# Attention into a mixture of four attention experts: both heads of a row through DRAM in one tile

## The chip, the cores and the metric

One core of one Trainium2 chip. The metric is the device time of one execution in microseconds (us), given as the median of several runs. The engines are TensorE (PE, with its weight loads as PEld), VectorE (DVE), ScalarE (ACT), GpSimd (POOL) and SyncE (SP), which here issues every DMA; its queue is SPq in the trace.

## The reference

Everything is float32. Causal attention over 8 heads with a window of 128 and 4 sink columns gives x; x goes through four experts of attention, whose outputs are weighted by the two best gates of each position.

```python
scores = scale * np.matmul(q, k.transpose(0, 1, 3, 2))          # q, k, v: (4, 8, 768, 64)
scores = np.where(is_sink | in_window, scores, -1e9)            # window 128, 4 sinks
a = softmax(scores); attn = np.matmul(a, v)
x = attn.transpose(0, 2, 1, 3).reshape(4, 768, 512)
...
logits = x @ w_gate; topk = the two largest of the 4 logits; w = softmax(their logits)
for e in range(4):
    q, k, v = x @ wq[e], x @ wk[e], x @ wv[e]                   # (4, 768, 64)
    a = softmax(where(causal, scale * q @ k.T, -1e9))
    ye = a @ v @ wo[e]
    out += (weight of e at this position, 0 if not chosen) * ye
```

## The kernel before

The work is cut into units. A unit `first(b, hp)` is the windowed attention of one batch and one pair of heads (16 of them), a unit `second(b, ep)` is the causal attention of one batch and one pair of experts (8 of them), with `values` (the projections of the values and the gates) before and `store` (the output projection) behind. The two heads or experts of a pair sit in the two halves of PE's rows, so one step does both. A unit has 6 rows of 128 positions; row i of a `second` sees i + 1 blocks of 128 columns. The stages of one such row in `wide_rows`: scores on PE (L1358), mask and minimum on DVE (L1571), exponential on ACT (L1579), sum and reciprocal (`factor`, L1413 to L1422), normalisation on POOL or ACT (`scaled`, L1238 or L1236), turning of the probabilities, product with the values on PE (`acc.add`, L1397), finisher.

The turning is done by PE with an identity (L1430) and copied out of PSUM, except in the rows named by `AWAY`: rows 3, 4 and 5 of the units (0,0), (0,1), (1,0), (1,1) and (2,0). Those go through DRAM in `by_way_of_dram`: for each of the two heads, the normalised probabilities are written in another order of columns into a tile `u` of the ring "p", DVE transposes it in blocks of 32 x 32 (L1523), one DMA writes it to a DRAM tile `there` (L1524), and four DMAs read it back so that the blocks of 32 rows change places (L1518). PE then multiplies with it directly, without transposes or copies.

Scores and trips share the ring "p" of 13 tiles of 768 columns; `there` is a ring of 4 tiles in DRAM, one per head.

The program of each engine is a list in a fixed order. `Plan.emit` makes it: each piece of work is a `Step` with a priority, modelled costs per engine it may run on, the steps it comes after and the ring buffers it takes or uses. `emit` goes through modelled time, gives each engine the step that can begin first (on PE: the least of priority plus `HURRY` times the wait, plus `STAY` and `BULK` terms where the tile mode changes), and writes the steps out in that order. `NUDGE` is a table of some 3000 numbers that shift the priorities of groups and of single steps, `ONLY` is a table that ties steps to one engine. On SP a step's `moves` is the modelled time that its bytes take. Where the model sees a gap on PE in the first 130 us, `fill` puts dummy products in (L1045). At run time the engines follow their lists and wait for each other by semaphores, so a wait in front of one instruction holds up all that stands behind it on its engine.

Of the kernel before, what the change touches and what calls it, by code (L numbers as in the profile page):

```python
# [39 lines left out]

FREE = {PE: 1100.0, DVE: 4500.0, ACT: 2100.0, POOL: 5300.0, SP: 790.0}

NUDGE = {
    "busy_PE": -19.1, " ": 0.5, " busy_PE": 42.4, " busy_PE 0": -148.0, "sink_values_DVE": 84.9, " sink_values_DVE": 10.8,
    " sink_values_DVE 0": -114.0, "load_SP": 37.3, " load_SP": 4.4, " load_SP 0": 5.1, "again_SP": 20.0, " again_SP": -6.7,
    "sink_values_ACT": -13.2, " sink_values_ACT": -20.4, " sink_values_ACT 0": 41.8, "sink_values_POOL": -7.2,
    " sink_values_POOL": 9.3, " sink_values_POOL 0": 10.1, "sink_values_SP": -9.6, " sink_values_SP": -26.6,
    " sink_values_SP 0": 39.2, " load_SP 1": -28.6, " weight_ACT": -0.4, " weight_ACT 0": 9.4, "weight_POOL": 6.6,
    " weight_POOL": -1.7, " weight_POOL 0": -35.7, " weight_ACT 1": 23.3, " weight_POOL 1": -20.8, " weight_ACT 2": 25.1,
# [1933 lines left out]
```

## Time and profile before

| what | value |
|---|---|
| median of 3 runs | 392.97 us (389.96 to 392.98) |
| the profiled execution | 394.25 us, its span 392.5 us |
| mean granted PE clock | 0.972 of full speed |
| busy, share of the span | PE 94%, PEld 81%, DVE 73%, ACT 70%, POOL 50% |
| HBM read and written | 30.88 and 16.12 MB |
| DMA issues through DRAM | 30 writes `there<-p`, 120 reads `p<-there` |

The span runs from the first to the last instruction of the profiled execution. A group's row has its busy time in us, the mean duration of one instruction in ns, and the idle time of the engine just before its instructions with what ended that. A busy PE is not PE at its peak, since the ends of matmuls are modelled.

### The profile page before, as it was taken

Reading aid. Unit: us, or ns where it says so; the run is one execution under the profiler, and the core shown is the slowest. Engines: PE = TensorE matmul, PEld = TensorE weight load, DVE = VectorE, ACT = ScalarE, POOL = GpSimd, SP = SyncE. Lnnn points to the kernel's source line nnn. Section 1 sums busy time; section 2 is a strip of 40 time slices with the busy share of each in tenths; the row PEclk is TensorE's granted clock in tenths of the full one; section 3 lists DMA queues with packets and bytes.
Section 4 is the critical chain, followed back from the end, with each engine's and each line's share of the span. In section 5 each row is a group of like instructions: output and inputs, shape, how many; then the busy total and the mean of one; then the engine's idle time right before and its main releaser. Section 6 shows DMA issues by size and latency. Waiting matters only on the chain.

```text
span 392.5 us, 13096 instructions
## 1 busy us (share of the span) xinstructions
PE 367.4 (94%) x4648; PEld 318.2 (81%) x4648; DVE 287.8 (73%) x1263; ACT 275.5 (70%) x950; POOL 196.0 (50%) x476
## 2 busy tenths in 40 slices
...
GB/s 165 205 154 151 161 188 171 115 0 130 212 198 112 124 243 152 91 60 301 198 156 136 135 222 154 19 3 183 249 177 2 3 28 28 2 1 109 3 55 109
DMA packets 145634, 48.13 MB, mean 123 GB/s; under 512 B 122976, under 2 KB 138336, under 8 KB 145568
## 3 DMA queue, kind: packets, MB, share of 16 engines
...
q8 instruction: 37, 0.61, 0.7%
q14 instruction: 29, 0.24, 0.2%
HBM read 30.88 MB, written 16.12 MB: 120 GB/s over the span
## 4 chain that ended last, share of the span: by engine, by line
PE 57%; DMA 12%; SPq 10%; DVE 9%; ACT 6%; issue 3%; POOL 2%; DVEq 0%; ACTq 0%; POOLq 0%
PE b L1397 12%; PE b L1800 10%; PE b L1874 9%; PE b L1827 8%; PE b L1358 6%; PE b L1430 6%; SPq L1518 5%; SPq L1768 3%; DMA qn<-in_q_dram 3%; DMA there<-p 3%; PE b L1371 2%; DMA p<-there 2%; PE b L1353 2%; ACT p L1579 1%; DVE p L1571 1%
## 5 line engine op out<-in xcount | busy, mean ns | idle before, releaser
L1579 ACT ACTIVATE p<-p,st 128x128 f32<-128x128 f32 (+5 forms) x96 | 63.7, 666 | 6.1 <-DVE st L1571 4.8
L1709 ACT ACTIVATE p<-p,st 128x132 f32<-128x132 f32 x128 | 50.7, 401 | 9.3 <-DVE st L1705 9.1
L1571 DVE CUSTOM_DVE_ANT_0 p<-b,cmask 128x384 f32<-128x384 f32 (+3 forms) x96 | 45.5, 502 | 2.3 <-PE b L1358 1.9
L1358 PE MATMUL b<-ks,qs 64*128 64x384 f32 (+3 forms) x384 | 44.4, 349 | 0.8 <-DVE y L1215 0.6
L1430 PE MATMUL b<-ident,p 64*128 64x64 f32 x820 | 40.1, 229 | 4.7 <-DVE st L1705 2.6
L1430 PEld LDWEIGHTS b<-ident,p 64*128 64x128 f32 x820 | 33.8, 141 | 10.9 <-issue 3.2
L1227 ACT ACTIVATE pt<-b 128x256 f32<-128x256 f32 (+3 forms) x102 | 38.7, 417 | 5.3 <-PE b L1430 4.5
L1397 PE MATMUL b<-pt,vn 128*64 128x128 f32 x448 | 41.2, 289 | 0.4 <-ACT pt L1227 0.4
L1413 POOL TENSOR_TENSOR st<-st 128x4 f32<-128x4 f32 (+1 forms) x57 | 11.3, 200 | 56.7 <-ACT p L1579 34.6
L1827 PE MATMUL b<-wvh,x 128*128 128x260 f32 x192 | 37.6, 286 | 0.2 <-DVE x L1215 0.2
L1358 PEld LDWEIGHTS b<-ks,qs 64*128 64x128 f32 x384 | 32.6, 194 | 4.0 <-issue 0.8
L1238 POOL TENSOR_SCALAR p<-p,st 128x640 f32<-128x640 f32 (+5 forms) x54 | 34.8, 655 | 1.9
L1874 PE MATMUL b<-woh,y 128*128 128x512 f32 x96 | 34.9, 399 | 0.0
L1487 POOL TENSOR_SCALAR_AFFINE_SELECT pt<-pt 128x512 f32<-128x512 f32 x32 | 20.3, 636 | 28.8 <-ACT pt L1227 20.4
L1727 POOL TENSOR_TENSOR p<-p,st 128x512 f32<-128x512 f32 x32 | 33.2, 1042 | 0.0
L1229 DVE COPY pt<-b 128x384 f32<-128x384 f32 (+3 forms) x72 | 31.7, 463 | 1.4 <-PE b L1430 1.0
L1800 PE MATMUL b<-x,wqh 128*128 128x256 f32 (+1 forms) x128 | 32.7, 341 | 0.0
L1705 DVE CUSTOM_DVE_ANT_0 p<-b,pair_mask 128x132 f32<-128x132 f32 x128 | 32.5, 284 | 0.1
L1800 PE MATMUL b<-x,wkh 128*128 128x512 f32 (+1 forms) x128 | 32.4, 339 | 0.0
L1827 PEld LDWEIGHTS b<-wvh,x 128*128 128x128 f32 x192 | 30.6, 188 | 1.5 <-issue 0.5
L1648 ACT ACTIVATE p<-p,st 128x128 f32<-128x128 f32 (+1 forms) x64 | 28.7, 450 | 3.3 <-DVE st L1643 3.3
L1236 ACT ACTIVATE p<-p,st 128x256 f32<-128x256 f32 (+5 forms) x42 | 26.1, 653 | 6.6 <-POOL st L1422 6.6
...
## 6 DMA issues: line engine op xcount, KB each, us to landing
vn<-in_v_dram SPq DMA_DIRECT2D x32, 192.0 KB, 3.5
...
qn<-in_q_dram SPq DMA_DIRECT2D x52, 96.0 KB, 3.3
kn<-in_k_dram SPq DMA_DIRECT2D x52, 96.0 KB, 2.6
there<-p SPq DMA_DIRECT2D x10, 384.0 KB, 4.1
p<-there SPq DMA_DIRECT2D x40, 96.0 KB, 2.3
...
```

What stands on the lines that cost most here:

```text
L1227: nc.scalar.activation(dst(), src(), AF.Copy)
L1238: nc.gpsimd.tensor_scalar(dst(), src(), by(), 1.0, op0=OP.mult, op1=OP.mult)
L1358: nc.tensor.matmul(o, self.qs.t[hs, a, qs], keys(hs, b), start=n == 0, stop=n == 2)
L1397: nc.tensor.matmul(o[e * 64:e * 64 + 64], lhs, rhs, start=e not in self.begun, stop=last and self.done == len(self.steps))
L1430: nc.tensor.transpose(t[g].t[:, n, :], x[gs], ident[gs, gs])
L1571: nc.vector.tensor_tensor_reduce(out=one(e)[:, cs], in0=s2[e].t[:, :(c1 - c0) * 128], in1=mask(c0, c1), scale=times, scalar=st.t[:, 3, es] ...
L1579: nc.scalar.activation(x, x, AF.Exp, bias=st.t[:, 0, es], scale=-1.0, accum_out=st.t[:, 1, es])
L1709: nc.scalar.activation(p.t[:, n, :], p.t[:, n, :], AF.Exp, bias=st.t[:, 0, n:n + 1], scale=-1.0, accum_out=st.t[:, 1, n:n + 1])
L1727: nc.gpsimd.tensor_mul(p.t[:, :, :128], p.t[:, :, :128], f()[:, :, None].to_broadcast([128, 4, 128]))
L1800: nc.tensor.matmul(t.t, w[a][:, c, es], X[b, c].t[:, x, cs], start=c == 0 and m == 0, stop=c == NCH - 1 and m == 2)
L1827: nc.tensor.matmul(t.t[:, :VW], X[b, c].t[:, a, qs], W["wv"][w][:, c, :], start=c == 0 and n == 0, stop=c == NCH - 1 and n == 2)
L1874: nc.tensor.matmul(t.t, Y[b, c].t[:, a, qs], W["wo"][w][:, c, :], start=c == 0 and n == 0, stop=c == EP - 1 and n == 2)
```

## The change

`by_way_of_dram` uses one tile `u` for both heads, from a ring of its own (3 tiles of 1536 columns), and "p" goes from 13 to 8 tiles. Both heads' normalisations write into `u`, whose columns are ordered block of 32, head, rest; two transposes, each of half the columns (so of both heads), come after both normalisations; one DMA writes the whole tile to a `there` of 1536 columns (still 4 of them); four DMAs read it back. The products read the same numbers from the other places. In the order's model each SP step's cost is multiplied by `ISSUE` = 1.2, and six other costs are set anew. The tables `NUDGE` and `ONLY`, and `HURRY`, `STAY` and `BULK`, are new; of the 2901 names that stand in both `NUDGE` tables 6 have the same number.

```diff
+ISSUE = 1.2
-HURRY = 72.48
-STAY = 79.02
-BULK = -16.1
+HURRY = 79.02
+STAY = 46.95
+BULK = 0.96
...
-            s.eng, s.begun, s.end = e, t, t + s.cost[e]
+            s.eng, s.begun, s.end = e, t, t + s.cost[e] * (ISSUE if e == SP else 1.0)
...
-             "p": (13, 768, F32),
-             "there": (4, 768, F32),
+             "p": (8, 768, F32), "u": (3, 1536, F32),
+             "there": (4, 1536, F32),
...
-        s = plan.step(prio, {POOL: 170 + 0.85 * n, ACT: 187 + 0.833 * n}, norm, after, new, use)
+        s = plan.step(prio, {POOL: 240 + 0.833 * n, ACT: 187 + 0.833 * n}, norm, after, new, use)
...
-        made = plan.step(prio, {DVE: 80, POOL: 150}, total, after, (), [st])
-        s = plan.step(prio, {DVE: 100}, inverse, [made], (), [st])
+        made = plan.step(prio, {DVE: 75, POOL: 150}, total, after, (), [st])
+        s = plan.step(prio, {DVE: 82}, inverse, [made], (), [st])
...
-        below_own = plan.step(prio, {POOL: 540}, tri, moved, (), [pt])
+        below_own = plan.step(prio, {POOL: 602}, tri, moved, (), [pt])
...
-            normed.append(plan.step(prio - LEAD_N, {POOL: 2 * (140 + 0.85 * (z - a)), ACT: 2 * (187 + 0.833 * (z - a))}, norm, [f], (), [p, st]))
+            normed.append(plan.step(prio - LEAD_N, {POOL: 2 * (235 + 0.84 * (z - a)), ACT: 2 * (187 + 0.833 * (z - a))}, norm, [f], (), [p, st]))
...
-                logits.append(plan.step(prio, {DVE: 210}, sort, [last], ...
+                logits.append(plan.step(prio, {DVE: 280}, sort, [last], ...
```

`by_way_of_dram` after, up to the products:

```python
        n = len(cols)
        u, there, normed = buf("u", 4, 2, n * 32), buf("there", 2 * n * 128), []
        for e in range(2):
            normed.append(scaled(prio - WIDE_N, lambda e=e: u.t[:, :, e, :].rearrange("p b (j c) -> p j b c", c=32),
                                 lambda e=e: one(e).rearrange("p (j b c) -> p j b c", b=4, c=32), 128 * n,
                                 lambda e=e: st.t[:, 2, e:e + 1], [r], [] if e else [u], [ps[e], st] + ([u] if e else [])))
        turns = []
        for h in range(2):
            def turn(x=lambda h=h: u.t[:, 2 * h:2 * h + 2].rearrange("p b e x -> p (b e x)")):
                nc.vector.transpose(x(), x())
            turns.append(plan.step(prio - WIDE_N, {DVE: 83 + 1.04 * 128 * n}, turn, normed, (), [u]))
        whole = lambda: u.t.rearrange("p b e x -> p (b e x)")
        s = plan.step(prio - WIDE_N, {SP: 430}, lambda: nc.sync.dma_start(there.t, whole()), turns, [there], [u], moves=330 * n)

        def back():
            for b in range(4):
                nc.sync.dma_start(u.t[32 * b:32 * b + 32].rearrange("r a e x -> r a (e x)"),
                                  there.t.rearrange("(a r) (b x) -> b r a x", a=4, b=4)[b])
        got = plan.step(prio - WIDE_N - 10, {SP: 1900}, back, [s], (), [there, u], moves=2 * MOVE * n)
        ...
                    acc.add(i, e, value[0](j, e), u.t[:, :, e, 32 * c:32 * c + 32], c == n - 1)
```

## Rows read from the trace of the kernel before

**Rows 1.** The page's first part: busy time of each engine, its share of the span and its instructions.

```profile
PE 367.4 (94%) x4648; PEld 318.2 (81%) x4648; DVE 287.8 (73%) x1263; ACT 275.5 (70%) x950; POOL 196.0 (50%) x476
```

**Rows 2.** Stretches of the span: start and end, length, busy time of PE, PEld, DVE, ACT and POOL with instructions, granted PE clock, DMA engines' share, GB/s.

```profile
0.00:90.00 90.00, 80.65 (x1116) 68.82 (x1118) 65.52 (x331) 63.55 (x252) 61.37 (x139) 0.94 0.76 143
90.00:125.00 35.00, 31.58 (x408) 26.96 (x410) 28.73 (x125) 28.14 (x103) 18.22 (x48) 0.95 0.75 177
125.00:165.00 40.00, 38.06 (x546) 33.55 (x543) 34.93 (x153) 35.96 (x128) 24.71 (x58) 1.00 0.62 154
165.00:215.00 50.00, 47.06 (x528) 41.03 (x527) 38.07 (x161) 29.78 (x103) 24.14 (x59) 0.97 0.67 167
215.00:255.00 40.00, 36.91 (x471) 32.05 (x468) 32.48 (x133) 29.53 (x99) 21.29 (x52) 0.96 0.49 130
255.00:300.00 45.00, 44.38 (x559) 38.80 (x557) 32.48 (x154) 29.72 (x112) 18.54 (x50) 1.00 0.42 133
300.00:392.50 92.50, 88.80 (x1040) 77.04 (x1036) 55.64 (x214) 58.82 (x160) 27.70 (x71) 0.99 0.10 36
```

**Rows 3.** The waits of PE, the first two: tile and line waited at, who ended the wait; total us, times, longest us.

```profile
PE b L1397 <- DMA p<-there: 7.7, 7, 1.5
PE b L1430 <- DVE st L1705: 3.6, 4, 2.3
```

**Rows 4.** PE in order of time, the products with a tile from DRAM (start, us, line, shapes, count; in brackets the idle time before them and its releaser). Each is named `p,v`.

```profile
115.25 1.51 PE L1397 MATMUL b<-p,v 128*64 128x128 f32 x23 [0.81 <-DMA p<-there]
...
120.56 0.40 PE L1397 MATMUL b<-p,v 128*64 128x128 f32 x2 [1.54 <-DMA p<-there]
121.57 1.73 PE L1397 MATMUL b<-p,v 128*64 128x128 f32 x13 [0.61 <-DMA p<-there]
...
152.39 1.53 PE L1397 MATMUL b<-p,v 128*64 128x128 f32 x24 [0.81 <-DMA p<-there]
...
155.55 1.27 PE L1397 MATMUL b<-p,v 128*64 128x128 f32 x16 [0.97 <-DMA p<-there]
...
214.17 1.04 PE L1397 MATMUL b<-p,v 128*64 128x128 f32 x16
...
245.23 0.40 PE L1397 MATMUL b<-p,v 128*64 128x128 f32 x2 [1.42 <-DMA p<-there]
247.13 1.33 PE L1397 MATMUL b<-p,v 128*64 128x128 f32 x14 [1.49 <-DMA p<-there]
```

**Rows 5.** Two stretches around waits of rows 4, columns as in rows 2.

```profile
118.00:126.00 8.00, 5.85 (x76) 5.06 (x74) 3.83 (x14) 3.37 (x12) 3.33 (x9) 0.79 0.74 133
246.00:252.00 6.00, 4.87 (x54) 4.38 (x56) 2.20 (x10) 2.35 (x9) 0.83 (x2) 0.72 0.05 13
```

**Rows 6.** SP's issues by line, with the least, the median and the greatest time of one in ns and the first and last start: reads from DRAM, writes to it, loads of values; and the page's lines with the size of such a load and of a write and a read of the widest rows (KB, median us to landing).

```profile
L1518 SPq DMA_DIRECT2D p<-there x120: 303/430/1902, 95.4 to 290.8; - x120
L1524 SPq DMA_DIRECT2D there<-p x30: 320/350/1497, 93.0 to 286.8; - x30
L1764 SPq DMA_DIRECT2D vn<-in_v_dram x32: 384/491/1940, 5.0 to 291.9; - x32
...
vn<-in_v_dram SPq DMA_DIRECT2D x32, 192.0 KB, 3.5
...
there<-p SPq DMA_DIRECT2D x10, 384.0 KB, 4.1
p<-there SPq DMA_DIRECT2D x40, 96.0 KB, 2.3
```

**Rows 7.** SP's issues in order of time (start, us from the first to the end of the last of the group, line, count).

```profile
109.55 1.93 SPq L1518 DMA_DIRECT2D p<-there  x4
111.53 3.37 SPq L1768 DMA_DIRECT2D kn<-in_k_dram  x4
114.94 5.08 SPq L1518 DMA_DIRECT2D p<-there  x8
...
147.01 6.94 SPq L1518 DMA_DIRECT2D p<-there  x12
...
217.92 3.15 SPq L1524 DMA_DIRECT2D there<-p  x2
...
237.54 0.85 SPq L1524 DMA_DIRECT2D there<-p  x2
241.68 3.64 SPq L1518 DMA_DIRECT2D p<-there  x8
```

**Rows 8.** Groups by line and shape (busy us, mean ns of one, idle before): the transposes of the widest and the narrowest row, the normalisation of 128 columns on POOL, the triangle on POOL.

```profile
L1523 DVE STREAM_TRANSPOSE p<-p 128x768 f32<-128x768 f32 x10 | 9.5, 962 | 0.1
L1523 DVE STREAM_TRANSPOSE p<-p 128x512 f32<-128x512 f32 x10 | 6.7, 681 | 1.7 <-ACT p L1236 1.7
L1238 POOL TENSOR_SCALAR p<-p,st 128x128 f32<-128x128 f32 x10 | 3.7, 376 | 0.4
L1487 POOL TENSOR_SCALAR_AFFINE_SELECT pt<-pt 128x512 f32<-128x512 f32 x32 | 20.3, 636 | 28.8 <-ACT pt L1227 20.4 <-DVE pt L1229 8.2
```

**Rows 9.** Stretches for the share of the DMA engines, columns as in rows 2.

```profile
95.00:100.00 5.00, 5.00 (x106) 4.33 (x101) 5.00 (x23) 5.00 (x15) 4.61 (x11) 1.00 0.98 237
115.00:120.00 5.00, 3.77 (x60) 3.39 (x60) 4.01 (x21) 3.89 (x17) 3.89 (x13) 1.00 0.45 103
180.00:185.00 5.00, 5.00 (x74) 4.17 (x73) 4.67 (x12) 4.26 (x12) 3.12 (x7) 1.00 1.00 387
```

**Rows 10.** The dummy products, a group by line and shape.

```profile
L1045 PE MATMUL b<-nought 128*64 128x128 f32 x112 | 8.3, 285 | 0.0
```

More of the change, by code (lines that the diff above doesn't have):

```diff
@@ L722 @@
+    "by_way_of_dram_SP": -23.0, "001 by_way_of_dram_SP": -34.5, "001 by_way_of_dram_SP 0": 119.6, "back_SP": -13.2,
[495 rows of a table added]
 }
 ONLY = {
[L725 to L728 removed]
@@ new lines @@
+    "010 fn_DVEACT 5": ACT, "010 fn_DVEACT 6": DVE, "010 fn_DVEACT 7": ACT, "010 total_DVEPOOL 0": POOL,
+    "010 norm_POOLACT 0": ACT, "010 fn_DVEACT 8": ACT, "010 fn_DVEACT 9": ACT, "010 fn_DVEACT 11": ACT,
+    "010 fn_DVEACT 12": ACT, "010 fn_DVEACT 13": ACT, "010 total_DVEPOOL 2": DVE, "010 fn_DVEACT 15": DVE,
+    "010 fn_DVEACT 16": ACT, "010 fn_DVEACT 17": ACT, "020 fn_DVEACT 0": ACT, "020 fn_DVEACT 1": DVE,
+    "020 fn_DVEACT 2": ACT, "020 fn_DVEACT 4": DVE, "020 fn_DVEACT 5": DVE, "020 fn_DVEACT 6": DVE, "020 fn_DVEACT 7": ACT,
@@ new lines @@
+    "020 norm_POOLACT 1": POOL, "020 fn_DVEACT 9": ACT, "020 total_DVEPOOL 1": DVE, "020 fn_DVEACT 11": DVE,
+    "020 fn_DVEACT 12": ACT, "020 fn_DVEACT 13": ACT, "020 fn_DVEACT 17": DVE, "030 fn_DVEACT 2": ACT,
+    "030 fn_DVEACT 4": ACT, "030 fn_DVEACT 6": ACT, "030 total_DVEPOOL 0": DVE, "030 norm_POOLACT 0": ACT,
+    "030 norm_POOLACT 1": ACT, "030 fn_DVEACT 8": ACT, "030 fn_DVEACT 9": DVE, "030 fn_DVEACT 10": ACT,
+    "030 fn_DVEACT 13": DVE, "030 fn_DVEACT 15": ACT, "030 fn_DVEACT 16": DVE, "110 total_DVEPOOL 0": POOL,
@@ new lines @@
+    "110 norm_POOLACT 1": ACT, "110 fn_DVEACT 0": DVE, "110 fn_DVEACT 1": ACT, "110 total_DVEPOOL 1": POOL,
+    "110 fn_DVEACT 3": DVE, "110 fn_DVEACT 4": ACT, "110 fn_DVEACT 5": DVE, "110 total_DVEPOOL 2": POOL,
+    "110 fn_DVEACT 6": ACT, "110 fn_DVEACT 7": DVE, "110 fn_DVEACT 9": ACT, "100 norm_POOLACT 0": ACT,
+    "100 norm_POOLACT 1": POOL, "100 fn_DVEACT 0": DVE, "100 fn_DVEACT 2": ACT, "100 fn_DVEACT 4": DVE,
+    "100 fn_DVEACT 5": ACT, "100 fn_DVEACT 6": DVE, "100 fn_DVEACT 9": DVE, "001 fn_DVEACT 0": ACT, "001 fn_DVEACT 1": DVE,
@@ new lines @@
+    "001 fn_DVEACT 2": ACT, "001 fn_DVEACT 3": ACT, "001 fn_DVEACT 4": DVE, "001 fn_DVEACT 5": DVE,
+    "001 total_DVEPOOL 0": DVE, "001 norm_POOLACT 1": ACT, "001 total_DVEPOOL 1": POOL, "001 total_DVEPOOL 2": DVE,
+    "001 norm_POOLACT 4": POOL, "001 fn_DVEACT 6": ACT, "001 norm_POOLACT 6": POOL, "001 total_DVEPOOL 4": POOL,
+    "001 norm_POOLACT 8": ACT, "001 total_DVEPOOL 5": DVE, "001 norm_POOLACT 10": ACT, "001 norm_POOLACT 11": ACT,
+    "001 fn_DVEACT 10": ACT, "120 total_DVEPOOL 0": DVE, "120 norm_POOLACT 1": ACT, "120 fn_DVEACT 0": DVE,
@@ new lines @@
+    "011 norm_POOLACT 8": POOL, "011 norm_POOLACT 9": ACT, "011 fn_DVEACT 2": DVE, "011 fn_DVEACT 3": ACT,
+    "011 norm_POOLACT 11": ACT, "011 fn_DVEACT 4": ACT, "011 fn_DVEACT 6": ACT, "011 fn_DVEACT 7": DVE,
+    "011 fn_DVEACT 8": ACT, "011 fn_DVEACT 11": DVE, "210 norm_POOLACT 0": ACT, "210 fn_DVEACT 0": ACT,
+    "210 fn_DVEACT 1": ACT, "210 total_DVEPOOL 1": POOL, "210 fn_DVEACT 2": DVE, "210 fn_DVEACT 4": ACT,
+    "210 fn_DVEACT 5": ACT, "210 total_DVEPOOL 2": POOL, "210 fn_DVEACT 6": DVE, "210 fn_DVEACT 8": ACT,
@@ new lines @@
+    "200 total_DVEPOOL 0": POOL, "200 norm_POOLACT 0": POOL, "200 norm_POOLACT 1": POOL, "200 fn_DVEACT 0": ACT,
+    "200 fn_DVEACT 1": ACT, "200 total_DVEPOOL 1": DVE, "200 fn_DVEACT 2": DVE, "200 fn_DVEACT 3": ACT,
+    "200 fn_DVEACT 5": ACT, "200 fn_DVEACT 6": DVE, "200 fn_DVEACT 7": DVE, "101 fn_DVEACT 2": DVE, "101 fn_DVEACT 4": ACT,
+    "101 fn_DVEACT 5": ACT, "101 total_DVEPOOL 1": DVE, "101 norm_POOLACT 2": ACT, "101 norm_POOLACT 3": POOL,
+    "101 total_DVEPOOL 2": POOL, "101 norm_POOLACT 4": POOL, "101 fn_DVEACT 7": ACT, "101 total_DVEPOOL 3": POOL,
@@ new lines @@
+    "101 norm_POOLACT 6": POOL, "101 norm_POOLACT 7": ACT, "101 norm_POOLACT 9": POOL, "101 fn_DVEACT 8": ACT,
+    "101 total_DVEPOOL 5": POOL, "101 norm_POOLACT 10": POOL, "101 norm_POOLACT 11": ACT, "101 fn_DVEACT 11": DVE,
+    "220 total_DVEPOOL 0": DVE, "220 norm_POOLACT 1": POOL, "220 fn_DVEACT 0": DVE, "220 fn_DVEACT 1": ACT,
+    "220 total_DVEPOOL 1": DVE, "220 fn_DVEACT 4": ACT, "220 fn_DVEACT 7": DVE, "220 fn_DVEACT 9": ACT,
+    "230 fn_DVEACT 1": ACT, "230 total_DVEPOOL 1": POOL, "230 fn_DVEACT 2": DVE, "230 total_DVEPOOL 2": DVE,
@@ new lines @@
+    "111 fn_DVEACT 10": DVE, "300 total_DVEPOOL 0": POOL, "300 norm_POOLACT 0": POOL, "300 fn_DVEACT 1": ACT,
+    "300 fn_DVEACT 2": DVE, "300 fn_DVEACT 3": ACT, "300 fn_DVEACT 4": ACT, "300 fn_DVEACT 5": DVE,
+    "300 total_DVEPOOL 2": POOL, "300 fn_DVEACT 7": DVE, "300 fn_DVEACT 8": DVE, "201 fn_DVEACT 0": ACT,
+    "201 fn_DVEACT 1": DVE, "201 fn_DVEACT 2": ACT, "201 fn_DVEACT 3": DVE, "201 fn_DVEACT 5": DVE,
+    "201 norm_POOLACT 0": ACT, "201 norm_POOLACT 1": ACT, "201 total_DVEPOOL 1": POOL, "201 norm_POOLACT 3": POOL,
@@ new lines @@
+    "201 norm_POOLACT 4": POOL, "201 norm_POOLACT 5": POOL, "201 fn_DVEACT 6": ACT, "201 total_DVEPOOL 3": DVE,
+    "201 norm_POOLACT 6": POOL, "201 norm_POOLACT 7": ACT, "201 total_DVEPOOL 4": POOL, "201 norm_POOLACT 8": ACT,
+    "201 norm_POOLACT 9": ACT, "201 fn_DVEACT 8": ACT, "201 fn_DVEACT 9": ACT, "201 total_DVEPOOL 5": POOL,
+    "201 norm_POOLACT 10": ACT, "201 fn_DVEACT 11": DVE, "310 fn_DVEACT 0": ACT, "310 fn_DVEACT 1": ACT,
+    "310 total_DVEPOOL 1": POOL, "310 fn_DVEACT 2": ACT, "310 fn_DVEACT 3": ACT, "310 fn_DVEACT 5": DVE,
@@ new lines @@
+    "310 fn_DVEACT 6": ACT, "310 fn_DVEACT 7": DVE, "310 fn_DVEACT 8": DVE, "320 fn_DVEACT 0": DVE,
+    "320 total_DVEPOOL 1": POOL, "320 fn_DVEACT 2": ACT, "320 fn_DVEACT 4": ACT, "320 fn_DVEACT 5": ACT,
+    "320 total_DVEPOOL 2": POOL, "320 fn_DVEACT 6": ACT, "320 fn_DVEACT 7": ACT, "320 fn_DVEACT 8": ACT,
+    "320 fn_DVEACT 9": DVE, "330 total_DVEPOOL 0": DVE, "330 norm_POOLACT 1": ACT, "330 fn_DVEACT 0": DVE,
+    "330 fn_DVEACT 1": ACT, "330 total_DVEPOOL 1": POOL, "330 total_DVEPOOL 2": DVE, "330 fn_DVEACT 6": ACT,
@@ new lines @@
+    "330 fn_DVEACT 7": DVE, "330 fn_DVEACT 8": ACT, "211 norm_POOLACT 1": POOL, "211 fn_DVEACT 0": DVE,
+    "211 fn_DVEACT 1": DVE, "211 total_DVEPOOL 1": DVE, "211 norm_POOLACT 2": POOL, "211 norm_POOLACT 3": POOL,
+    "211 fn_DVEACT 2": DVE, "211 norm_POOLACT 5": POOL, "211 fn_DVEACT 5": DVE, "211 total_DVEPOOL 3": POOL,
+    "211 norm_POOLACT 7": ACT, "211 fn_DVEACT 7": ACT, "211 total_DVEPOOL 4": POOL, "211 norm_POOLACT 9": ACT,
+    "211 fn_DVEACT 8": DVE, "211 fn_DVEACT 10": DVE, "211 fn_DVEACT 11": ACT, "211 norm_POOLACT 11": POOL,
@@ new lines @@
+    "211 fn_DVEACT 12": DVE, "211 fn_DVEACT 14": DVE, "211 fn_DVEACT 16": DVE, "211 fn_DVEACT 17": DVE,
+    "211 fn_DVEACT 19": ACT, "211 fn_DVEACT 20": DVE, "301 fn_DVEACT 1": DVE, "301 total_DVEPOOL 0": POOL,
+    "301 norm_POOLACT 0": ACT, "301 norm_POOLACT 1": ACT, "301 fn_DVEACT 6": DVE, "301 fn_DVEACT 7": ACT,
+    "301 total_DVEPOOL 1": POOL, "301 norm_POOLACT 2": POOL, "301 fn_DVEACT 8": DVE, "301 fn_DVEACT 9": ACT,
+    "301 total_DVEPOOL 2": POOL, "301 norm_POOLACT 4": ACT, "301 fn_DVEACT 10": ACT, "301 fn_DVEACT 11": DVE,
@@ new lines @@
+    "301 norm_POOLACT 6": ACT, "301 norm_POOLACT 7": ACT, "301 fn_DVEACT 12": DVE, "301 fn_DVEACT 13": DVE,
+    "301 total_DVEPOOL 4": POOL, "301 fn_DVEACT 15": DVE, "301 fn_DVEACT 17": ACT, "301 norm_POOLACT 10": ACT,
+    "301 fn_DVEACT 18": ACT, "301 fn_DVEACT 20": ACT, "311 norm_POOLACT 0": POOL, "311 fn_DVEACT 0": DVE,
+    "311 fn_DVEACT 1": DVE, "311 total_DVEPOOL 1": POOL, "311 norm_POOLACT 2": ACT, "311 fn_DVEACT 2": DVE,
+    "311 norm_POOLACT 5": ACT, "311 fn_DVEACT 4": ACT, "311 total_DVEPOOL 3": DVE, "311 norm_POOLACT 6": POOL,
@@ new lines @@
+    "311 norm_POOLACT 7": POOL, "311 fn_DVEACT 6": DVE, "311 fn_DVEACT 8": DVE, "311 fn_DVEACT 9": ACT,
+    "311 fn_DVEACT 10": ACT, "311 fn_DVEACT 11": ACT, "311 total_DVEPOOL 5": POOL, "311 norm_POOLACT 10": ACT,
+    "311 norm_POOLACT 11": ACT, "311 fn_DVEACT 12": DVE, "311 fn_DVEACT 14": DVE, "311 fn_DVEACT 15": ACT,
+    "311 fn_DVEACT 16": DVE, "311 fn_DVEACT 17": ACT, "311 fn_DVEACT 19": ACT, "311 fn_DVEACT 20": ACT,
+    "311 fn_DVEACT 21": ACT,
+}
+HURRY = 79.02
+STAY = 46.95
+BULK = 0.96
@@ L1509, in by_way_of_dram @@
     def by_way_of_dram(prio, acc, i, one, ps, cols, r, st, value):
-        n, got, us = len(cols), [], []
+        n = len(cols)
+        u, there, normed = buf("u", 4, 2, n * 32), buf("there", 2 * n * 128), []
         for e in range(2):
-            u, there = buf("p", n * 128), buf("there", n * 128)
-            us.append(u)
-            def back(u=u, there=there):
-                for b in range(4):
-                    nc.sync.dma_start(u.t[32 * b:32 * b + 32].rearrange("r (a x) -> r a x", a=4),
-                                      there.t.rearrange("(a r) (b x) -> b r a x", a=4, b=4)[b])
-            s = scaled(prio - WIDE_N, lambda u=u: u.t.rearrange("p (b j c) -> p j b c", b=4, c=32),
-                       lambda e=e: one(e).rearrange("p (j b c) -> p j b c", b=4, c=32), 128 * n,
-                       lambda e=e: st.t[:, 2, e:e + 1], [r], [u], [ps[e], st])
-            s = plan.step(prio - WIDE_N, {DVE: 83 + 1.04 * 128 * n}, lambda u=u: nc.vector.transpose(u.t, u.t), [s], (), [u])
-            s = plan.step(prio - WIDE_N, {SP: 420}, lambda u=u, there=there: nc.sync.dma_start(there.t, u.t), [s], [there], [u], moves=165 * n)
-            got.append(plan.step(prio - WIDE_N - 10, {SP: 1900}, back, [s], (), [there, u], moves=MOVE * n))
@@ new lines, in by_way_of_dram @@
+            normed.append(scaled(prio - WIDE_N, lambda e=e: u.t[:, :, e, :].rearrange("p b (j c) -> p j b c", c=32),
+                                 lambda e=e: one(e).rearrange("p (j b c) -> p j b c", b=4, c=32), 128 * n,
+                                 lambda e=e: st.t[:, 2, e:e + 1], [r], [] if e else [u], [ps[e], st] + ([u] if e else [])))
+        turns = []
+        for h in range(2):
+            def turn(x=lambda h=h: u.t[:, 2 * h:2 * h + 2].rearrange("p b e x -> p (b e x)")):
+                nc.vector.transpose(x(), x())
+            turns.append(plan.step(prio - WIDE_N, {DVE: 83 + 1.04 * 128 * n}, turn, normed, (), [u]))
```

121 lines of the change are left out of this document (26 added, 95 removed), and 1334 rows, old and new, of the table NUDGE.

## Prediction

> **What bounds the kernel now.** I read the page's first lines, then the stretches, then who TensorE waited for. TensorE (PE) is busy 367.4 of 392.5 us [rows 1], so 25.1 us is all that any change of waits can win from idle time. Cut by stage [rows 2], that idle time is 9.4 us before 90 us (loads, first pairs), 3.4 in 90 to 125, 1.9 in 125 to 165, 2.9 in 165 to 215, 3.1 in 215 to 255, 0.6 in 255 to 300, 3.7 after. The trips through DRAM lie in 90 to 295 us, one burst of three rows (six heads) for each of five units; outside them the edit proper touches nothing but buffers. The largest named cause is the one the change is about: 7.7 us in 7 waits of the products with the values (L1397) for the tile that comes back from DRAM, ahead of 3.6 us for a softmax reduction [rows 3]. The waits sit in three of the five bursts: 0.81 + 1.54 + 0.61 = 2.96 us around 115 to 122, 0.81 + 0.97 = 1.78 us around 152 to 156, 1.42 + 1.49 = 2.91 us around 245 to 247 [rows 4]. The other two bursts cost PE nothing.
>
> A wait costs more than itself. Behind the pauses of 118 to 122 and 245 to 247 the granted clock is 0.79 over 118 to 126 and 0.72 over 246 to 252 [rows 5]: 8 x 0.21 = 1.7 and 6 x 0.28 = 1.7 us of full-speed time lost, a fall to the lower level (1.2 GHz) in part of each stretch. So the bursts cost PE at most 7.7 + 3.4 = 11.1 us, an upper bound for the edit's own gain.
>
> **The change, part by part.** *Transfers.* Per row 2 writes to DRAM and 8 reads become 1 and 4, twice as large. On SP a read costs 0.430 us to issue and a write 0.350 (medians of 120 and 30) [rows 6]. Gone are 60 x 0.430 + 15 x 0.350 = 31.1 us of SP's queue, 2.07 us per row. A median leaves out the issues of up to 1.9 us in the same row, so this is a lower bound, provided that an issue costs the same when its pieces are twice as long. The count of pieces per read stays (32 partitions x 4), and a load of values of 192 KB issues in 0.491 us where a read of at most 96 KB takes 0.430 [rows 6], so I take the same; at the other end, an issue in proportion to bytes, the gain would be nil.
>
> *Where this is on the path.* Only where SP is still issuing when PE is ready. Burst 1: SP issues the last two heads' reads from 114.94 for 5.08 us; before them stand four loads for keys (3.37 us) and four reads (1.93 us) [rows 7]. Eight issues become four: 2.5 us earlier. The first 8 reads of the burst lose as much, which moves the key loads too. Wait there 2.96: I take 2.5 off. Burst 2: twelve reads from 147.01 last 6.94 us, 3 heads [rows 7]; in whole rows they become eight at most, so the last tile is at least 4 x 0.43 = 1.7 us earlier, and I let the whole 1.78 go. Burst 4: two writes at 237.54, landed 4.1 us later at 241.68, then eight reads in 3.64 us [rows 7]. Four issues go, 1.8 us, but two things come in.
>
> *What comes in.* (a) Both blocks of transposes now wait for both heads' normalisation; before, the first head's could run under the second's. One transpose takes 0.68 to 0.96 us [rows 8], so the last write starts later by 0 (the two were back to back anyway) to 0.96; I take 0.5. If the list puts a transpose too early, DVE stands still at it, and with it the masks (L1571) and copies behind, which PE needs; the list is made from modelled ends, so I count nothing more. (b) One write of twice the bytes. 384 KB more [rows 6] at the best rate seen, 387 GB/s in 180 to 185 [rows 9], is 1.0 us; where the two old writes were in flight together it is nothing. I take 0.5 of 0 to 1.0. Together 1.0 of 0 to 2.0, against 2.07 us of issue. So for a single row in an empty queue the edit is nearly neutral; its gain is in queues that are full. Burst 4 thus gives 1.8 - 1.0 = 0.8 off 2.91, while in bursts 1 and 2 the 1.0 eats what is beyond the waits and some 0.5 of burst 1. Sum over bursts: 2.0 + 1.8 + 0.8 = 4.6 us.
>
> *Clock.* With burst 1's waits nearly gone its fall of 1.7 us goes; burst 4's stays. Bounds 0 and 3.4, I take 1.7: burst 4 keeps 2.1 us of pause, the row it resembles.
>
> *Buffers.* Scores had 13 tiles of 768, shared with the trips; now 8, with 3 of 1536 for trips. While six trip tiles were out, 7 were left, so a burst has one more. Each unit has three rows, so a row of the next unit must wait for a product of the last unit. The tightest pair is 214.17 (last product of the third burst, 1.04 us [rows 4]) against 217.92 (first write of the fourth [rows 7]): the third slot is not needed before the fourth burst's third row, about 10 to 20 us later (237.54). So nothing. After 300 us no trips exist and 5 tiles fewer are there; PE has 3.7 us of idle time in those 92.5 us [rows 2]. Four wide rows in flight instead of six: taken at 0, and up to 2 if it bites. DRAM slots hold 4 rows instead of 4 heads, which can only help.
>
> *VectorE, ScalarE, GpSimd, PE.* The count and size of the normalisations, transposes and products don't change; they read four runs of 32 columns as before. Taken at 0.
>
> *The order made anew.* Every nudge and most engine choices are new, and the weights of the order's choice on PE too (a change of tile mode now costs 46.95 instead of 79.02). This touches the 25.1 - 7.7 = 17.4 us of other idle time and the 8.3 us of dummy products that fill planned gaps [rows 10]. In its favour the model's costs move toward the trace: a 128-wide normalisation on GpSimd from 279 to 347 ns (the trace has 376), the triangle from 540 to 602 (636) [rows 8], four read issues from 1.9 to 2.28 us (4 x 0.43 = 1.72 by the median, 1.93 to 5.08 / 2 = 2.54 by the runs of rows 7). Against it: the trace of before shows nothing of the new order. A third of 17.4 either way is a large shift for a list that does the same work; I take 0 with bounds of -5 and +6.
>
> **Sum.** 394.25 us is the profiled execution's own time (span 392.5 and 1.75 around it); it is 1.3 above the median of 392.97. 394.25 - 4.6 - 1.7 = 387.95. On the median's scale 386.7. I forecast 387.5.
>
> **A rule against it.** Between 95 and 100 us the DMA engines are 0.98 busy, and 1.00 in 180 to 185 [rows 9]: bytes, not issues, could hold the transfers, and the bytes stay. "DMA: Bandwidth & Descriptors" of the Trainium skill, section "Issuing engines are not separate DMA queues", says that issuing time is usually small beside the DMA itself; by that the change would bring nothing. The trace agrees for one transfer (0.43 us of issue) and not for a burst of them, where SP issues back to back.
>
> **The rivals.** *Same time.* The engines' share, not SP, sets when a tile lands, or the freed queue lets the q and k loads in earlier and these take the engines from the reads. For: the shares above. Against: in 115 to 120, while SP still issues and PE waits, the share is 0.45 [rows 9]. Then the 4.6 and the 1.7 stay, and the order gives or takes 3: 390 to 396, centre 393.
>
> *Slower: a longer chain per row.* Place: the last row of each burst. Price: +0.96 (transposes), +1.0 to 4.1 (a write that takes as long again as the 4.1 us of today, if landing goes with bytes [rows 6]), -2.07. At the worst +3.0 us a burst, exposed in four or five of them since the new order places the products as tightly as the old: 12 to 15 us, less the 4.6 that full queues give, plus one or two falls of the clock at 1.7. That is 394.25 + 10 = about 402 (398 to 407). It decides once a double write lands over 2.1 us later than a single one. Against: bursts 3 and 5 had slack, and the planner counts the doubled bytes.
>
> *Not what it says:* that the new order, not the transfers, makes the difference. It has the same sum with the order's term alone, -5 to +6, so 389 to 400; it lies inside the other cases.
>
> **How the numbers follow.** Forecast (queues shorten, order neutral or better) 0.55, own range 381 to 391; same time 0.24; slower 0.21. A change within 1% (389 to 397) can hardly be told from none here. Faster by over 1%: 0.50 of the forecast's 0.55 and 0.02 of the second case, 0.52; slower by over 1%: 0.18 of the slower case's 0.21 and 0.02 of the second, 0.20; within 1%: the other 0.28. The range must leave out 2 in 10: from 380 (387.95 with the order's -5 and the other fall of the clock gone, 381.3, less 1.3 for the median) to 399 (the near part of the slower case).
>
> **What would show it.** In the profile after: 60 reads and 15 writes with medians near 0.43 and 0.35 us; PE's waits for the tile from DRAM down from 7.7 to about 3 us, with the burst around 245 keeping most of that; PE idle near 19 us; the granted clock's mean a little over 0.972. Wrong would make it: read issues nearer 0.9 us, writes landing over 5 us, new PE waits on the three trip tiles or on scores, or an idle total outside the bursts that moved by more than 5 us.

## The result and the profile after

The changed kernel takes 381.43 us (median of 4 runs, 380.89 to 383.07) against 392.98: a ratio of 0.9717 [0.9643, 0.9791], 11.55 us faster where 5.5 was forecast. The sign and the range held. The profiled execution took 381.89 us, its span 379.1 us. All ratios, and the 384.11 us of one kernel below, leave out executions in a slower state that the chip has at times.

The page's first line, busy time of each engine, beside [rows 1]:

```profile
PE 360.7 (95%) x4642; PEld 310.3 (82%) x4642; DVE 292.6 (77%) x1272; ACT 271.0 (71%) x943; POOL 196.3 (52%) x474
```

The span fell by 392.5 - 379.1 = 13.4 us. PE was busy 367.4 - 360.7 = 6.7 us less, and idle 25.1 - 18.4 = 6.7 us less: two equal halves. The first fits the clock: its mean went from 0.972 to 0.989, and (1 - 0.972) x 392.5 = 11.0 us of full-speed time lost became (1 - 0.989) x 379.1 = 4.2, 6.8 less. (The profiled execution of the kernel before has a low clock for that kernel: on the first chip of the experiments the medians are 0.978 and 0.990, and this half is nearer 5 us.) The stretches, columns as in [rows 2]:

```profile
0.00:90.00 90.00, 83.16 (x1178) 70.55 (x1178) 71.97 (x356) 65.21 (x257) 65.76 (x149) 0.96 0.77 147
90.00:125.00 35.00, 32.45 (x452) 26.66 (x450) 31.14 (x140) 28.19 (x104) 20.81 (x51) 1.00 0.71 171
125.00:165.00 40.00, 38.18 (x469) 34.12 (x466) 32.87 (x144) 28.95 (x107) 19.75 (x53) 1.00 0.68 159
165.00:215.00 50.00, 48.24 (x658) 41.47 (x656) 42.98 (x181) 41.52 (x140) 29.00 (x68) 1.00 0.68 173
215.00:255.00 40.00, 38.30 (x385) 33.45 (x381) 28.44 (x114) 23.01 (x75) 17.00 (x44) 1.00 0.51 134
255.00:300.00 45.00, 45.00 (x702) 39.38 (x701) 39.89 (x186) 39.95 (x157) 28.92 (x73) 1.00 0.40 116
300.00:379.10 79.10, 75.40 (x818) 64.73 (x816) 45.27 (x159) 44.17 (x109) 15.05 (x42) 0.99 0.11 41
```

From 90 us to 300 us the clock is 1.00 in every stretch, where [rows 2] has 0.95 to 0.97 in three of the five. PE's idle time went from 9.4 to 6.8 us before 90 us, where no trip through DRAM has begun, from 12.0 to 7.8 between 90 and 300, and stayed at 3.7 after 300. So 2.5 us of the idle half came from a stretch that the transfers do not touch. What PE waited for, the first two of the list, as in [rows 3]:

```profile
PE b L1392 <- DMA u<-there: 6.8, 5, 1.9
PE b L1425 <- ACT pt L1222: 1.6, 2, 0.9
```

The waits for the tile from DRAM, which the change was forecast to cut from 7.7 us to about 3, are 6.8 us. PE in order of time, the products with such a wait, as in [rows 4]:

```profile
113.09 1.09 PE L1392 MATMUL b<-u,v 128*64 128x128 f32 x16 [1.93 <-DMA u<-there]
144.01 1.53 PE L1392 MATMUL b<-u,v 128*64 128x128 f32 x24 [0.53 <-DMA u<-there]
147.49 1.09 PE L1392 MATMUL b<-u,v 128*64 128x128 f32 x16 [1.29 <-DMA u<-there]
200.88 1.09 PE L1392 MATMUL b<-u,v 128*64 128x128 f32 x16 [1.40 <-DMA u<-there]
233.14 1.53 PE L1392 MATMUL b<-u,v 128*64 128x128 f32 x24 [1.66 <-DMA u<-there]
```

By burst they went from 2.96, 1.78, 0 and 2.91 us to 1.93, 1.82, 1.40 and 1.66. So of the 13.4 us, 0.9 came from the waits that the change was about, 5.8 from other idle time (17.4 to 11.6) and 6.7 from PE's busy time. The gain did not come by the road of the prediction. SP's issues and the sizes and landings on the page, as in [rows 6]:

```profile
L1522 SPq DMA_DIRECT2D u<-there x60: 303/432/1662, 98.4 to 271.0; - x60
L1518 SPq DMA_DIRECT2D there<-u x15: 326/349/459, 93.0 to 263.6; - x15
...
there<-u SPq DMA_DIRECT2D x5, 768.0 KB, 4.1
u<-there SPq DMA_DIRECT2D x20, 192.0 KB, 5.1
there<-u SPq DMA_DIRECT2D x5, 640.0 KB, 2.9
u<-there SPq DMA_DIRECT2D x20, 160.0 KB, 3.8
```

An issue costs what it did at half the size (0.432 against 0.430, 0.349 against 0.350), so 31 us of SP's queue are gone as worked out. The widest write lands in 4.1 us as it did at half the size in the kernel before. But a read of 192 KB lands in 5.1 us where one of 96 KB took 2.3. For one row of the widest kind that undoes the saving. By these medians, from the first read's issue to the last one's landing, eight would take 7 x 0.43 + 2.3 = 5.3 us, and four 3 x 0.43 + 5.1 = 6.4. The traces, which have the landing of half of the reads, show the two nearer to each other: in the five widest rows the last landing that is there comes 6.4 us (median) after the first issue in the kernel after, and 6.2 with the old transfers in its lists (the second run below).

### The profile page after: what moved, and what is told of

Same layout as the page of the kernel before. It is cut to its first block, busy times and chain, and to the rows that moved or that the text cites. A ratio compares the mean times of both kernels' runs of the same rounds, so it can differ in the third digit from the quotient of the medians.

```text
span 379.1 us, 12937 instructions
## 1 busy us (share of the span) xinstructions
PE 360.7 (95%) x4642; PEld 310.3 (82%) x4642; DVE 292.6 (77%) x1272; ACT 271.0 (71%) x943; POOL 196.3 (52%) x474
## 4 chain that ended last, share of the span: by engine, by line
PE 63%; DMA 10%; DVE 9%; ACT 6%; SPq 5%; POOL 4%; issue 2%; DVEq 0%; ACTq 0%
PE b L1392 15%; PE b L1873 9%; PE b L1799 9%; PE b L1353 7%; PE b L1826 7%; PE b L1425 7%; DMA u<-there 4%; DMA qn<-in_q_dram 3%; SPq L1767 3%; PE b L1348 3%; PE b L1366 3%; DMA there<-u 3%; SPq L1522 2%; ACT p L1708 2%; DVE u L1515 2%
## 5 line engine op out<-in xcount | busy, mean ns | idle before, releaser
L1578 ACT ACTIVATE p<-p,st 128x640 f32<-128x640 f32 (+5 forms) x96 | 63.6, 665 | 14.2 <-DVE st L1570 11.4
L1392 PE MATMUL b<-pt,vn 128*64 128x128 f32 x448 | 39.0, 280 | 0.6 <-ACT pt L1222 0.5
L1224 DVE COPY pt<-b 128x256 f32<-128x256 f32 (+3 forms) x75 | 32.1, 450 | 8.3 <-PE b L1425 7.4
L1408 POOL TENSOR_TENSOR st<-st 128x2 f32<-128x2 f32 (+1 forms) x52 | 10.2, 197 | 51.7 <-ACT p L1578 27.9
L1873 PE MATMUL b<-woh,y 128*128 128x512 f32 x96 | 32.8, 400 | 0.0
L1799 PE MATMUL b<-x,wkh 128*128 128x256 f32 (+1 forms) x128 | 32.7, 343 | 0.0
L1647 ACT ACTIVATE p<-p,st 128x256 f32<-128x256 f32 (+1 forms) x64 | 28.6, 450 | 1.8 <-DVE st L1642 1.4
L1392 PEld LDWEIGHTS b<-pt,vn 128*64 128x64 f32 x448 | 25.4, 136 | 3.1 <-ACT pt L1222 0.8
L1366 PE MATMUL b<-kx,qn 64*64 64x196 f32 (+2 forms) x768 | 27.2, 286 | 0.0
L1826 PE MATMUL b<-wvl,x 128*128 128x260 f32 x96 | 27.1, 282 | 0.0
```

Of the source, the lines that this page charges most:

```text
L1366: nc.tensor.matmul(o, self.q_of()[hs, q0 + 64 * h:q0 + 64 * h + 64], ks, start=True, stop=True)
L1392: nc.tensor.matmul(o[e * 64:e * 64 + 64], lhs, rhs, start=e not in self.begun, stop=last and self.done == len(self.steps))
L1578: nc.scalar.activation(x, x, AF.Exp, bias=st.t[:, 0, es], scale=-1.0, accum_out=st.t[:, 1, es])
L1799: nc.tensor.matmul(t.t, w[a][:, c, es], X[b, c].t[:, x, cs], start=c == 0 and m == 0, stop=c == NCH - 1 and m == 2)
L1826: nc.tensor.matmul(t.t[:, :VW], X[b, c].t[:, a, qs], W["wv"][w][:, c, :], start=c == 0 and n == 0, stop=c == NCH - 1 and n == 2)
L1873: nc.tensor.matmul(t.t, Y[b, c].t[:, a, qs], W["wo"][w][:, c, :], start=c == 0 and n == 0, stop=c == EP - 1 and n == 2)
```

## The experiments

Three things changed at once: the transfers, the order's model, and the two tables. The runs take them apart. Ratios are to the kernel before, timed on the same chip; three chips were used, and it had a median of 392.3 us on each.

**The kernel after once more**, on the first chip of the experiments.

> The changed kernel as it is, timed beside the three others. All theories: 380 to 383 us, span about 379, the granted clock's mean near 0.99, PE's waits for the tile from DRAM near 7 us.

381.06 us, 0.9722 [0.9661, 0.9784]. It is the base for the runs below.

**Old transfers in the new lists.** The engines' lists are those of the kernel after; the one write becomes two and the four reads become eight, of the old sizes.

```diff
-        ... nc.sync.dma_start(there.t, whole()) ...
+                nc.sync.dma_start(there.t[:, x], whole()[:, x])       # for each half x
...
-                nc.sync.dma_start(u.t[32 * b:32 * b + 32].rearrange("r a e x -> r a (e x)"),
-                                  there.t.rearrange("(a r) (b x) -> b r a x", a=4, b=4)[b])
+                for e in range(2):
+                    nc.sync.dma_start(u.t[32 * b:32 * b + 32, :, e, :],
+                                      there.t.rearrange("(a r) (b e x) -> b e r a x", a=4, b=4, e=2)[b, e])
```

> The new order, instruction for instruction on PE, DVE, ACT and POOL, but each row's one write is two and its four reads are eight, each of the old size, at the same places of SP's list (75 issues more). Theory 1, the transfers won the time: 31 us of issue come back to SP and most of the gain goes: 387 to 392 us, PE waits for the tile from DRAM of 11 us or more. Theory 2, the new order won it and bytes set when a tile lands: 381 to 384 us, waits of 6 to 9 us.

390.02 us, 0.9950 [0.9909, 0.9990]: 9.0 us over the kernel after. PE's wait for the tile, SP's reads, the widest writes and reads with their time to landing, SP in order of time, and the first of these waits on PE (start, us, line, shapes, count, idle time before):

```profile
PE b L1392 <- DMA u<-there: 9.2, 6, 3.2
...
L1529 SPq DMA_DIRECT2D u<-there x120: 318/430/1522, 98.8 to 285.4; - x120
there<-u SPq DMA_DIRECT2D x10, 384.0 KB, 3.5
u<-there SPq DMA_DIRECT2D x40, 96.0 KB, 2.2
...
103.46 4.75 SPq L1529 DMA_DIRECT2D u<-there  x8
108.31 2.08 SPq L1774 DMA_DIRECT2D qn<-in_q_dram  x4
110.44 3.84 SPq L1529 DMA_DIRECT2D u<-there  x8
...
115.35 2.34 PE L1392 MATMUL b<-u,v 128*64 128x128 f32 x15 [3.25 <-DMA u<-there]
```

The widest reads land in 2.2 us and the tile is late all the same: SP issues without a pause from 103.46 us to 114.28, and PE stands still for 3.25 us in one piece behind this queue. In this list the 75 issues cost 9.0 us, net of the earlier landing of the smaller reads; the first theory had the time, and 11 us or more of waits where there are 9.2. Of the 9.1 us by which the spans differ, 2.4 stand at the tile, 2.2 in other idle time and 4.5 in PE's busy time, with the mean clock at 0.981. The new lists with the old transfers are thus 2.3 us below the kernel before.

**New transfers in the old lists.** PE, ACT and POOL keep the order of the kernel before, and so do DVE and SP but for the first head's transposes, write and reads: one merged set stands where the second head's stood. The merged tile lies in two neighbouring slots of "p" (14 slots, what 8 + 3 x 2 hold after).

```diff
+    big = consts.tile([128, 14 * 768], F32, name="big")
+    slots["p"] = [big[:, 768 * x:768 * x + 768] for x in range(14)]
+    slots["u"] = [big[:, 768 * x:768 * x + 1536] for x in range(14 - 1)]
...
+        for k, x in enumerate(ORDER):        # in emit: the list of the kernel before
```

> The old order, the same list on PE, ACT and POOL, with the change's transfers: both heads of a row in one tile (two neighbours of the ring p, which gets a 14th tile), the two transposes, the one write and the four reads each at the place where the later of the two heads' stood. Theory 1: most of the gain is here, 383 to 388 us, PE waits for the tile from DRAM down from 7.7 to about 3 us and a clock near 0.985. Theory 2: 390 to 395 us, waits of 6 to 9 us, clock as before near 0.972.

393.49 us, 1.0054 [1.0016, 1.0092]. The new transfers alone bring nothing; they cost half a per cent.

```profile
PE b L3178 <- DMA big<-there: 7.8, 4, 3.2
...
there<-big SPq DMA_DIRECT2D x5, 768.0 KB, 4.3
big<-there SPq DMA_DIRECT2D x20, 192.0 KB, 5.1
```

The wait is 7.8 us where [rows 3] has 7.7, in four pieces instead of seven, and the widest reads land in the 5.1 us of the kernel after.

**Both heads together, but transfers of the old size, in the old lists.** The kernel just told with the edit of the first experiment: two writes and eight reads per row, all where the second head's stood.

> As the old order with the change's tile, but two writes and eight reads per row, each of the old size: what the pairing of the heads alone does (the first head loses its head start) without the saved issues. Theory 1: 393 to 398 us, 5 us or more above the one with one write and four reads. Theory 2: within 2 us of that one.

408.84 us, 1.0398 [1.0311, 1.0485], slower than either case had it. Its two largest waits on PE and its widest writes and reads:

```profile
PE b L3178 <- DMA big<-there: 10.0, 7, 3.5
PE b L3211 <- DVE st L3497: 6.4, 4, 3.0
...
there<-big SPq DMA_DIRECT2D x10, 384.0 KB, 3.1
big<-there SPq DMA_DIRECT2D x40, 96.0 KB, 2.8
```

So in the old lists the change is a sum of two large terms: holding back the first head's transposes, write and reads costs 408.84 - 392.3 = 16.5 us, and the 75 issues less, net of the later landings, give 408.84 - 393.49 = 15.4 us back. Part of the 16.5 does not stand at the tile: 6.4 us of waits for a softmax reduction (L3497; 3.6 us in [rows 3]) say that DVE and the masks behind the transposes slipped too.

**Only the clock.** The kernel before, with zero products put on PE ahead of the last row's products in bursts 1 and 4, so that PE is not idle in those two waits.

```diff
+MORE = {("001", 3): 10, ("111", 3): 13}
...
+        more = MORE.get((plan.part, i), 0)
...
         def av():
             acc.done += 1
+            for _ in range(more):
+                for e in range(2):
+                    acc.add(i, e, nought[:, :64], nought)
```

> The kernel before with the same lists and one addition: 20 and 26 dummy products (of zeros, added to the sum) on PE in front of the products of row 3 in the first and the fourth burst, where PE stood still for the tile from DRAM and the granted clock then fell. Theory, the stillness costs the clock: the falls at 120 and 247 us go, PE's busy time beside the dummies drops by up to 3.4 us, 389 to 391 us. Rival, the clock falls for another reason or the products are late anyway: 392 to 395 us.

394.03 us, 1.0045 [0.9998, 1.0092]. The stretches of [rows 5] and the one before the second, PE's wait for the tile, and two places of PE's list:

```profile
118.00:126.00 8.00, 6.75 (x109) 5.95 (x109) 3.49 (x11) 3.71 (x12) 4.31 (x13) 1.00 0.73 135
240.00:246.00 6.00, 6.00 (x91) 5.87 (x89) 4.42 (x20) 4.03 (x10) 1.57 (x5) 0.87 0.41 121
246.00:252.00 6.00, 6.00 (x108) 5.66 (x106) 2.69 (x12) 2.23 (x10) 1.00 (x3) 1.00 0.02 4
...
PE b L1398 <- DMA p<-there: 1.4, 2, 1.1
...
126.14 0.58 PE L1431 MATMUL b<-ident,p 64*128 64x64 f32 x11 [1.25 <-DVE st L1577]
...
237.68 4.23 PE L1359 MATMUL b<-ks,qs 64*128 64x384 f32 x24
```

The same score products in the kernel before:

```profile
237.71 2.24 PE L1358 MATMUL b<-ks,qs 64*128 64x384 f32 x23
```

Where the clock was 0.79 and 0.72 it is 1.00; just before the second, 240 to 246, it is 0.87 (1.00 in the kernel before). The mean stays 0.972 and the time does not fall. What was won at the two places was lost beside them: behind the first, PE waits 1.25 us for a mask (L1577), a wait that the kernel before does not have, and ahead of the second, 24 score products take 4.23 us where 23 of them took 2.24 in the kernel before. So filling these two waits wins nothing in this list; that is no proof that the clock behind them was worth nothing.

**Half the bytes read back.** The kernel after, whose four reads fetch the first head's half only. It leaves out bringing back the second head's half.

```diff
-                nc.sync.dma_start(u.t[32 * b:32 * b + 32].rearrange("r a e x -> r a (e x)"),
-                                  there.t.rearrange("(a r) (b x) -> b r a x", a=4, b=4)[b])
+                nc.sync.dma_start(u.t[32 * b:32 * b + 32, :, 0, :],
+                                  there.t.rearrange("(a r) (b e x) -> b e r a x", a=4, b=4, e=2)[b, 0])
```

> The new kernel with the same lists and the same 60 reads, each of half the bytes: the second head's half of each tile isn't read back, so its blocks keep their places and the result is not the reference's. Theory, bytes set when a tile of the merged transfers lands: reads land in 2 to 3 us instead of 4 to 5, PE's waits for the tile fall from 6.8 to 1 to 3 us, 376 to 379 us. Rival, the issue and the wait for the write set it: waits of 5 to 7 us, 380 to 382 us.

372.62 us, 0.9527 [0.9471, 0.9582], 8.4 us below the kernel after. Its engines and its read's landing:

```profile
PE 356.9 (97%) x4642; PEld 307.7 (83%) x4642; DVE 292.1 (79%) x1272; ACT 270.3 (73%) x943; POOL 197.1 (53%) x474
...
u<-there SPq DMA_DIRECT2D x20, 96.0 KB, 2.9
```

No wait of PE for the tile is left. With the issues as few as they are now, the bytes of the reads are what the trips still cost: the 6.8 us of waits are most of the 8.4 (7.6 by the two ratios, since the kernels ran on different chips). That is more than the 2 to 5 us that were expected.

**Model and transfers apart, without the tables.** With empty tables (`NUDGE = {}`, `ONLY = {}`) the order can be made for each pairing of transfers and model (`ISSUE`, the six costs, `HURRY`, `STAY`, `BULK`). The four kernels:

```diff
-NUDGE = {...}
-ONLY = {...}
+NUDGE = {}
+ONLY = {}
```

Old transfers, old model:

> The old kernel with both tables of the order empty, with its old costs and weights: 405 to 430 us. Read beside the new kernel so treated.

New transfers, new model:

> The new kernel with both tables of the order empty, so that the model alone makes the lists, with the new costs and weights. If the tables carry the new order's gain: 405 to 430 us, and no better than the old kernel so treated. If the transfers and the model's costs carry it: 10 us or more below the old kernel so treated.

Old transfers, new model:

> Both tables empty, the old transfers (two writes and eight reads a row), but the new kernel's model: ISSUE of 1.2, the six new costs, the new HURRY, STAY and BULK. If a list made for the transfers needs the merged ones: 392 to 398 us, like the old kernel with empty tables (395.4). If the better model makes the better list: 384 to 389 us.

New transfers, old model:

> Both tables empty, the merged transfers, but the old model: ISSUE of 1, the old six costs, the old HURRY, STAY and BULK. If the merged transfers carry the gain once the list is made for them: 383 to 389 us. If the model does: 392 to 398 us.

| tables empty | old model | new model |
|---|---|---|
| old transfers | 395.42 us, 1.0124 [1.0042, 1.0206] | 380.78 us, 0.9714 [0.9650, 0.9777] |
| new transfers | 381.27 us, 0.9739 [0.9687, 0.9790] | 384.11 us, 0.9795 [0.9714, 0.9877] |

The new model alone gives 14.6 us, the new transfers alone 14.2, both together 11.3; the intervals of these three overlap. The old transfers under the new model are as fast as the kernel after, and both single changes are faster than was expected of them. What PE waits for at the tile from DRAM, in the four kernels in the order in which they are told above, and the engines of the third:

```profile
PE b L633 <- DMA p<-there: 4.8, 5, 1.5
```

```profile
PE b L635 <- DMA u<-there: 4.3, 3, 1.7
```

```profile
PE b L633 <- DMA p<-there: 0.8, 1, 0.8
...
PE 366.2 (97%) x4778; PEld 316.6 (83%) x4778; DVE 291.8 (77%) x1260; ACT 275.8 (73%) x969; POOL 189.8 (50%) x460
```

```profile
PE b L635 <- DMA u<-there: 1.7, 1, 1.7
```

A list in which eight small reads per row cost 0.8 us of waits exists, with PE idle for 379.4 - 366.2 = 13.2 us. (This idle time can't be set beside the 18.4 us of the kernel after: the empty tables leave larger planned gaps, and the dummy products in them keep PE busy for 16.2 us, against 8.2.) So the issues are no floor under the time: what they cost depends on the list. That the empty tables would cost tens of us was wrong: they cost 395.42 - 392.3 = 3.1 us in the old kernel and 384.11 - 381.06 = 3.1 in the new, the latter inside the two intervals.

**Fewer bytes, same result.** Of the 4 x 4 blocks that a row's reads move, the four on the diagonal stay where they are. The reads of the first and the last block of rows can leave theirs out and remain one transfer: 60 reads, an eighth fewer bytes, lists unchanged.

```diff
             for b in range(4):
-                nc.sync.dma_start(u.t[32 * b:32 * b + 32].rearrange("r a e x -> r a (e x)"),
-                                  there.t.rearrange("(a r) (b x) -> b r a x", a=4, b=4)[b])
+                a, z = int(b == 0), 4 - int(b == 3)
+                nc.sync.dma_start(u.t[32 * b:32 * b + 32, a:z].rearrange("r a e x -> r a (e x)"),
+                                  there.t.rearrange("(a r) (b x) -> b r a x", a=4, b=4)[b, :, a:z])
```

> The new kernel with the same lists, but the reads of the first and the last block of 32 rows leave out the piece that is where it belongs already: 60 reads as before, an eighth fewer bytes read back, the same numbers. Theory, bytes in the way of the landing: a quarter of what half the bytes gave (8.4 us), so 1.5 to 2.5 us, 378.5 to 379.5 us. Rival, the last of four reads sets the landing and it is a whole one in two of four: no change, 380.5 to 381.5 us.

376.08 us, 0.9593 [0.9546, 0.9639]: 5.0 us below the kernel after, twice what was expected, and the fastest kernel here that computes all of the reference.

```profile
PE b L1392 <- DMA u<-there: 1.3, 2, 0.8
...
u<-there SPq DMA_DIRECT2D x10, 192.0 KB, 4.6
u<-there SPq DMA_DIRECT2D x10, 144.0 KB, 4.0
```

The wait falls from 6.8 to 1.3 us. The widest reads land in 4.6 us where they stayed whole and in 4.0 where a quarter of them is left out, instead of 5.1. An eighth of the bytes gave 5.0 us where half of them gave 8.4, so the gain is not in proportion to the bytes. Leaving out the two inner diagonal blocks as well takes two transfers in place of one for each of the middle blocks: six reads per row, a quarter fewer bytes.

> As the last, and the two middle blocks leave their piece out too, which takes two reads each: six reads a row instead of four (30 issues more, 13 us of SP at 0.43), a quarter fewer bytes read back, the same numbers. If bytes weigh more than issues: 376 to 379 us. If issues weigh as the split of the transfers showed (75 issues more cost 9.0 us, so 30 cost 3.6): 379 to 382 us.

382.04 us, 0.9767 [0.9714, 0.9820]:

```profile
PE b L1392 <- DMA u<-there: 5.2, 4, 1.8
L1523 SPq DMA_DIRECT2D u<-there x90: 302/424/1778, 99.0 to 273.5; - x90
```

The 30 issues more, at a median of 0.42 us, lose what the bytes gave.

## Why the prediction was right in sign and wrong in its road

- **Issues.** Right: by the medians 31.1 us of SP's queue went, at unchanged cost per issue.
- **What comes in (b).** The step priced the write of double size, 0.5 us of 0 to 1.0. In the same lists it lands 0.6 us later (3.5 to 4.1 in the new) and 1.2 later (3.1 to 4.3 in the old), so that price was fair. It left out the reads of double size, and those land 2.8 us later (5.1 against 2.3). That is the term that failed: with it, four reads bring a widest row home no sooner than eight did (6.4 against 6.2 us in the new lists), and the 4.6 us off three bursts are not there: their waits fell by 2.2 us, and the third burst got one of 1.4. The merged kernel in the old lists shows the sum: +0.5% (1.2 us) where -6.3 was summed.
- **What comes in (a).** Taken at 0.5 us a row for the transposes' wait, with the step's own warning of masks that stand behind them counted at nothing. Both heads held together cost 16.5 us in the old lists, with DVE's wait and the first head's trip not told apart. Both of the terms that the sum set against each other were larger than thought there, and nearly equal: the issues gave 15.4 us where three bursts were to give 2.5 + 1.8 + 1.8 = 6.1.
- **The order made anew.** Taken at 0 with bounds of -5 and +6, as a term to be added to that of the transfers. The two do not add: the new transfers in the old lists are +1.2 us, the old transfers in the new lists -2.3, both together -11.2. For the merged transfers the new lists are worth 393.49 - 381.06 = 12.4 us, more than twice the bound. The rival "not what it says" named the right suspect, but the new order alone does not make the difference either. A third of the 17.4 us of other idle time was allowed to move, and 5.8 did; what the bound left out is the clock, on which the order bears too.
- **The clock.** 1.7 us forecast, 6.7 measured in the profiles (near 5 by the medians of the clock), and not in the way told: filling two waits by themselves brought no time. What the new list gains is spread over the span [rows 2], with the clock at 1.00 from 90 to 300 us.
- **The rule against it.** For the forecast transfers in the old lists the rule that the prediction took from the Trainium skill ("DMA: Bandwidth & Descriptors", section "Issuing engines are not separate DMA queues"), no gain, came nearer than the sum did in the total, +0.5% measured, but not in the cause. The runs disagree with it in both lists: 75 fewer issues gave 15.4 us in the old and 75 more cost 9.0 in the new.
- **The other rivals.** "Same time" is what the transfers alone did, with the later landing of the reads and the first head held back against the issues saved; whether the freed queue let the q and k loads in earlier was not tried. The longer chain per row was real (the reads' landing more than the write's), and the new list covered all but 6.8 us of it.
- **Buffers.** Taken at 0, as found: POOL and ACT, which write the three trip tiles, wait 1.6 us in all before they do, none of it for a product with such a tile, and PE's list names no wait for one to come free. PE's idle time, forecast near 19 us, is 18.4, and that is luck: the tile's waits kept 6.8 where 3 was told, and other idle time fell from 17.4 to 11.6.

**What stays open.** That the sign and the range held is in part luck too: the sum's gain was looked for at the tile, and 12.5 of the 13.4 us came from elsewhere. What makes these 12.5 us is not shown beyond this, that neither the transfers nor the lists alone bring them in the kernels with tables. Why the old transfers under the old model give the one slow list of the four is not shown. That the model's higher price of an issue keeps products further from their reads fits the 0.8 us, but the new transfers under the old model have 1.7 us without it. Four lists are few, lists differ by chance, and which of the model's changed numbers does it was not tried.
